# A fused attention and two-layer feed-forward kernel: all of w_in loaded ahead of w_out, and later keys and values loaded from GpSimd's queue

## The chip, the cores and the metric

One core of a Trainium2 chip runs the whole program. Times are device microseconds from start to end of one execution; the time of a kernel is the median of its runs. PE is TensorE (PEld its weight load), DVE is VectorE, ACT is ScalarE, POOL is GpSimd and SP is SyncE, which computes nothing here and starts DMA transfers. Each engine takes its own instructions strictly in order, and a transfer is started by an instruction in the queue of SP, ACT or POOL.

## The reference

Keys and values are averaged over groups of eight rows, then comes softmax attention, and two feed-forward layers follow it:

```python
B, H, S, D = 8, 8, 576, 64
k_p = k.reshape(B, H, 72, 8, D).mean(axis=3)
v_p = v.reshape(B, H, 72, 8, D).mean(axis=3)
attn = softmax(q @ k_p.transpose(0, 1, 3, 2) / sqrt(D))
x = (attn @ v_p) as 4608 tokens of 512
h = x @ w_in                         # 512 x 2048
x = (h * cos(h)) @ w_out             # 2048 x 512
g = x @ w_gate                       # 512 x 1536
out = (silu(g) * (x @ w_val)) @ w_out2
```

q, k and v are float32; the weights are float64.

## The kernel before

The program has two large stages. In the first, tokens go in nine blocks of 512 (`NB`), and each block in 16 slots (`NF1`): a slot computes 128 columns of h with twelve matmuls (`pe_h`, L507 to L509), its cosine on ACT and DVE (`turns`, `cosine`: L516, L518, L519, L540, L541, L544), and multiplies it with 128 rows of w_out into four accumulators (`pe_y`, L570 in block 0, L577 to L579 later). The attention of batch b + 1 is spread over slots of the blocks before it is needed. The second stage (the gate, value and output layers) is not touched here.

Ahead of slot 0 stands a prologue: the first batch's attention, written as a string of steps (`program`, L1057). In it `s`, `x`, `p`, `a` are scores, softmax, transposed probabilities and attention times values; `K0` to `K3` and `U0` are the second batch's sums of keys and values on DVE (L190, L192); `q` loads the second batch's q (four transfers, all on ACT's queue); `iN` loads N units of w_in, `oN` N units of w_out; `fN` takes N steps of weight conversion; `x4` is the softmax of the last tile; `k` prepares the second batch's keys; `b` starts the first load of batch 2's keys.

Weights are doubles and are turned into floats by hand: `cv_exp` (L445, takes the exponent), `cv_bias` (ACT, L451), `cv_sign` (L456), `cv_high` (L462), `cv_low` (L467), `cv_mul` (L473), and for w_in a split in a high and a low part (ACT L974, DVE L987). One unit of w_in or of w_out is 128 rows of 512 doubles, 512 KB; one of w_in comes as two transfers of 256 KB. The units are converted in a fixed sequence (`order`): w_in's first eight, then w_out's first, then one of w_in and one of w_out by turns. There are 16 of each. w_in's units are loaded straight into their homes (`wa00` to `wa33`), of which wa20 to wa22 and wa30 to wa33 hold the second batch's raw values and keys until their sums are done; w_out's units pass through two staging tiles (`raw`), so that the third waits for the first one's conversion.

From batch 2 on, keys and values come in 13 pieces a batch (8 of keys, 72 x 512 floats, 144 KB; 5 of values in two transfers each, 128 x 512 floats), through two tiles (tag `kv`, two buffers). `do_raw` starts the load of the next piece and then sums the present one on POOL (L190 twice, L192 once). Six batches make 108 such transfers. The sums of batch b go to a tile `kp` or `vp` that has one buffer, so they wait until PE has transposed the keys of the batch before (`prep_k`, L214), or until `prep_v` has read the values before. `prep_v(2)` writes into new tiles (`vmh_2`, `vml_2`, `vl2_2`), which POOL clears once with a MEMSET (L119); the one of `vmh_2` waits for PE's last use of the memory (L358), and ACT's L233 waits for that MEMSET.

The order of the instructions on each engine is set by the tile framework's scheduler when the program is built: it takes what is ready by its own estimates of time, and the written order as priority. On the chip the order is fixed.

Of the kernel before, what the change touches and what calls it, by code (L numbers as in the profile page):

```python
# [25 lines left out]
def fused_kernel(  # L26
# [18 lines left out]
    nc = tc.nc  # L45
# [7 lines left out]
    NP = H // 2  # L53
    SM = 64
# [102 lines left out]
    kview = [k[b].rearrange(pairs, r=2, l=POOL) for b in range(B)]  # L157
    vview = [v[b, :, : SM * POOL].rearrange(pairs, r=2, l=POOL) for b in range(B)]
    vleft = [v[b, :, SM * POOL :].rearrange("h (s l) d -> h s (l d)", l=POOL) for b in range(B)]

    def load_kv(b, kind, i):

        rows = SP if kind == "k" else P
        t = kvraw[b, kind, i] = p1a.tile([P, POOL * D], F32, name=f"{kind}raw_{b}_{i}", tag="kv", bufs=2)[:rows]
        if kind == "k":
            nc.sync.dma_start(t, kview[b][i % 2, :, i // 2])
        else:
            for r in range(2):
                nc.sync.dma_start(t[r * SM : (r + 1) * SM], vview[b][r, :, i] if i < NP else vleft[b])

    def load_kv1():

# [196 lines left out]
    def do_raw(b, i):  # L369
        at = (b - 2) * (H + NP + 1) + i  # L370
        if at + 1 < len(raws):
            load_kv(*raws[at + 1])
        sum_kv(*raws[at])
# [677 lines left out]
    def sum_v1():  # L1051
        new_vp(1)
        for j, t in vraw1:
# [1 line left out]


    program = (  # L1057
        "s0 s1 f4 x0 s2 p0 V0 v x1 p1 f3 s3 a0 x2 p2 f3 x3 i1 p3 a1 w F3 X s4 i1 q o2 "
        "K0 K1 K2 K3 U0 x4 k b i3 f6 "
    )  # L1060
    steps = {
        "s": s_,
# [11 lines left out]
        "q": lambda: load_q(1),  # L1074
        "k": lambda: prep_k(1),
        "b": lambda: load_kv(*raws[0]),
        "w": lambda: wo_raw.extend(
            p1w.tile([P, 8, DM], F32, name=f"wo_{i}", tag=f"big{i}", bufs=1) for i in range(2)
# [179 lines left out]
```

## Time and profile before

| | before |
|---|---|
| median of 3 runs | 1803.17 us (1802.95 to 1803.2) |
| the profiled execution | 1804.83 us, its span 1803.1 us |
| mean granted TensorE clock | 0.995 |
| PE busy | 1737.5 us (96%) |
| DVE, ACT, POOL busy | 1263.8 (70%), 1066.6 (59%), 171.7 (10%) |
| DMA | 357.01 MB, mean 198 GB/s |

The span is 1.7 us shorter than the execution, and the execution is 1.7 us longer than the median of the runs. PE's row in the profile's picture of 40 slices (45 us each) reads 2, 8, 7 and then nines: what PE does not use of the span lies in the first 130 us and in short gaps up to 320 us. In the same slices DVE reads 6 8 9 8 6 and POOL 0 1 5 0 5. A wait in the profile is put down to the instruction that ended it.

### The profile page before, as it was taken

The page shows a single profiled execution, that of the slowest core. Times are in us where ns is not written, and L with a number is a line of the kernel's source. Part 1 is how long each engine was busy: PE and PEld are TensorE (multiplying, and loading weights), DVE is VectorE, ACT ScalarE, POOL GpSimd, SP SyncE. Part 2 cuts the span into 40 slices and gives each one's busy share as a digit, 9 for nine tenths or more (in the row PEclk, how much of TensorE's full clock was granted, in tenths as well). Part 3 has the DMA queues.
Part 4 walks back from the last instruction along what each step waited for, and adds up shares of the span by engine and source line. Part 5 has one row for each costly group of instructions (what it writes and reads, how often), then busy time and mean ns, then how long its engine had stood idle before and what let it go on. Part 6 is the DMA issues. An engine that isn't in the chain of part 4 may idle for free.

```text
span 1803.1 us, 23421 instructions
## 1 busy us (share of the span) xinstructions
PE 1737.5 (96%) x8044; PEld 1439.4 (80%) x8044; DVE 1263.8 (70%) x2152; ACT 1066.6 (59%) x1933; POOL 171.7 (10%) x254
## 2 busy tenths in 40 slices
PE   2879999999999999999999999999999999999998
PEld 2546587888878888878877888888888888999998
DVE  6898688877877677787875586863584367358446
ACT  3578587777777767778776565533443344344333
POOL 0150513304104022000000000000000000000000
PEclk9989999999999999999999999999999999999999
DMA  9934246446566455474885488576667556787773
GB/s 186 203 104 120 79 165 188 156 131 197 148 205 218 114 198 144 158 220 153 235 275 176 159 320 291 193 252 225 194 200 267 193 192 221 290 265 246 294 249 93
DMA packets 248157, 357.01 MB, mean 198 GB/s; under 512 B 149608, under 2 KB 155752, under 8 KB 248040
## 3 DMA queue, kind: packets, MB, share of 16 engines
q1 hardware_dynamic: 224840, 352.58, 61.7%
q10 hardware_dynamic: 23200, 2.95, 1.1%
q8 instruction: 64, 1.05, 0.2%
q14 instruction: 53, 0.43, 0.1%
HBM read 285.74 MB, written 69.73 MB: 197 GB/s over the span
## 4 chain that ended last, share of the span: by engine, by line
PE 68%; DVE 14%; DMA 9%; ACT 5%; issue 2%; SPq 1%; POOL 0%; ACTq 0%; DVEq 0%
PE X L762 13%; PE oX L892 8%; PE Y L762 7%; PE h L507 4%; PE h L509 4%; PE h L508 4%; PE acc L578 4%; PE oY L892 4%; PE acc L579 4%; PE acc L577 4%; PE Z L762 3%; DMA w2r<-w_dram 2%; PE oZ L892 2%; PE av L358 2%; PE acc L570 2%
## 5 line engine op out<-in xcount | busy, mean ns | idle before, releaser
L762 PE MATMUL X<-t_P,wc 128*128 128x512 f32 (+1 forms) x1080 | 232.6, 367 | 1.0 <-ACT u L811 1.0
L507 PE MATMUL h<-xhl,wa 128*128 128x512 f32 x576 | 231.5, 402 | 0.0
L508 PE MATMUL h<-xhl,wa 128*128 128x512 f32 x576 | 226.3, 393 | 1.3 <-DVE xhl L131 1.3
L509 PE MATMUL h<-xhl,wa 128*128 128x512 f32 x576 | 225.6, 392 | 0.0
L762 PEld LDWEIGHTS X<-t_P,wc 128*128 128x128 f32 x1080 | 196.5, 188 | 27.5 <-ACT u L811 2.4
L578 PE MATMUL acc<-gl,wo_ring 128*128 128x512 f32 x448 | 176.4, 394 | 1.7 <-DVE gl L558 1.5
L577 PE MATMUL acc<-gh,wo_ring 128*128 128x512 f32 x448 | 175.1, 401 | 3.1 <-ACT gh L555 2.9
L579 PE MATMUL acc<-gh,wo_ring 128*128 128x512 f32 x448 | 175.4, 391 | 0.0
L544 DVE SCALAR_TENSOR_TENSOR w<-w,hs 128x512 f32<-128x512 f32 x144 | 102.3, 710 | 49.7 <-ACT w L541 48.4
L516 ACT ACTIVATE hs<-h 128x512 f32<-128x512 f32 x144 | 85.7, 595 | 76.4 <-DVE w L544 47.8
L540 ACT ACTIVATE w<-w 128x512 f32<-128x512 f32 x144 | 91.0, 632 | 64.9 <-DVE w L519 63.8
L507 PEld LDWEIGHTS h<-xhl,wa 128*128 128x128 f32 x576 | 108.7, 189 | 25.7 <-issue 4.1
L508 PEld LDWEIGHTS h<-xhl,wa 128*128 128x128 f32 x576 | 108.7, 189 | 25.3 <-issue 2.4
L509 PEld LDWEIGHTS h<-xhl,wa 128*128 128x128 f32 x576 | 108.5, 188 | 23.8 <-issue 0.9
L519 DVE SCALAR_TENSOR_TENSOR w<-w,hs 128x512 f32<-128x512 f32 x144 | 105.3, 731 | 23.7 <-ACT w L518 23.5
L814 DVE TENSOR_TENSOR p<-p,X 128x512 f32<-128x512 f32 (+1 forms) x60 | 37.9, 632 | 117.0 <-PE X L762 109.5
L558 DVE TENSOR_TENSOR gl<-w,gh 128x512 fp32r<-128x512 f32 x128 | 90.9, 710 | 40.2 <-ACT gh L555 38.6
L130 ACT CAST xhl<-pst 128x1024 fp32r<-128x1024 f32 (+1 forms) x70 | 67.7, 967 | 71.3 <-PE oX L892 26.1
L518 ACT ACTIVATE w<-hs,few 128x512 f32<-128x512 f32 x144 | 104.5, 725 | 7.3 <-DMA w_dram<-ce_w 4.2
L892 PE MATMUL oX<-xhl,wc 128*128 128x512 f32 (+1 forms) x480 | 102.8, 368 | 0.0
L578 PEld LDWEIGHTS acc<-gl,wo_ring 128*128 128x128 f32 x448 | 84.6, 189 | 21.5 <-DVE gl L558 5.2
L577 PEld LDWEIGHTS acc<-gh,wo_ring 128*128 128x128 f32 x448 | 84.1, 189 | 21.7 <-ACT gh L555 4.9
(197 smaller groups left out, 3586.3 us busy)
## 6 DMA issues: line engine op xcount, KB each, us to landing
wc<-wc_dram SPq DMA_DIRECT2D x273, 512.0 KB
wo_ring<-wo_dram SPq DMA_DIRECT2D x112, 512.0 KB
wc_dram<-wc SPq DMA_DIRECT2D x42, 512.0 KB
wc_dram<-ow SPq DMA_DIRECT2D x42, 256.0 KB
y_dram<-yo SPq DMA_DIRECT2D x18, 512.0 KB
w_dram<-ce_w SPq DMA_DIRECT2D x36, 256.0 KB
st_i<-in_moe_w_in_dram SPq DMA_DIRECT2D x32, 256.0 KB
st_o<-in_moe_w_out_dram SPq DMA_DIRECT2D x16, 512.0 KB
```

What stands on the lines that cost most here:

```text
L507: nc.tensor.matmul(ps, whi, xhl[:, 0, c], start=c == 0, stop=False)
L508: nc.tensor.matmul(ps, whi, xhl[:, 1, c], start=False, stop=False)
L509: nc.tensor.matmul(ps, wlo, xhl[:, 0, c], start=False, stop=c == KC - 1)
L518: nc.scalar.activation(w, h, AF.Identity, bias=magic)
L519: nc.vector.scalar_tensor_tensor(out=w, in0=w, scalar=MAGIC, in1=h, op0=ALU.subtract, op1=ALU.subtract)
L540: nc.scalar.activation(w, w, AF.Sin, scale=PI)
L544: nc.vector.scalar_tensor_tensor(out=w, in0=w, scalar=1.0, in1=h, op0=ALU.subtract, op1=ALU.mult, reverse0=True)
L577: nc.tensor.matmul(acc[n][i], a[:, cols], xh, start=f == 0, stop=False)
L578: nc.tensor.matmul(acc[n][i], a[:, cols], xl, start=False, stop=False)
L579: nc.tensor.matmul(acc[n][i], b[:, cols], xh, start=False, stop=f == NF1 - 1)
L762: nc.tensor.matmul(ps[:, :hb], w, t[:, x, c, :hb], start=first and c == 0 and n == 0, stop=c == 1 and n == 2, skip_group_check=not first,)
L892: nc.tensor.matmul(banks[key][m][:, :hb], u, x[:, b, i, :hb], start=first_ and j == i == k == 0, stop=j == NJ - 1 and i == 1 and k == 2, s ...
```

## The change

Three lines change. The step `i11` loads all that is left of w_in behind the second batch's sums and ahead of `o2`, which before stood ahead of the sums with `i3` behind `b`; the loads that the slots of block 0 issued one by one find nothing left to do. And `load_kv`, which loads the pieces of keys and values of batches 2 to 7, issues from POOL's queue and not from SP's.

```diff
     def load_kv(b, kind, i):
         rows = SP if kind == "k" else P
         t = kvraw[b, kind, i] = p1a.tile([P, POOL * D], F32, ..., tag="kv", bufs=2)[:rows]
         if kind == "k":
-            nc.sync.dma_start(t, kview[b][i % 2, :, i // 2])
+            nc.gpsimd.dma_start(t, kview[b][i % 2, :, i // 2])
         else:
             for r in range(2):
-                nc.sync.dma_start(t[r * SM : (r + 1) * SM], vview[b][r, :, i] if i < NP else vleft[b])
+                nc.gpsimd.dma_start(t[r * SM : (r + 1) * SM], vview[b][r, :, i] if i < NP else vleft[b])
...
     program = (
-        "s0 s1 f4 x0 s2 p0 V0 v x1 p1 f3 s3 a0 x2 p2 f3 x3 i1 p3 a1 w F3 X s4 i1 q o2 "
-        "K0 K1 K2 K3 U0 x4 k b i3 f6 "
+        "s0 s1 f4 x0 s2 p0 V0 v x1 p1 f3 s3 a0 x2 p2 f3 x3 i1 p3 a1 w F3 X s4 i1 q "
+        "K0 K1 K2 K3 U0 i11 o2 x4 k b f6 "
     )
```

SP's queue behind w_in's eighth unit (`st_i1_3`), before. `st_o0_0` and `st_o0_1` are w_out's first two units, `kraw_2_0` the first keys of batch 2, `st_i2_0` w_in's ninth unit; `DMAHW` names the semaphore of an earlier transfer that has to have landed.

```order
L438 DMA st_i1_3_432<-in_moe_w_in_dram 64x512 [waits DMAHW6_49]
L438 DMA st_o0_0_440<-in_moe_w_out_dram 128x512 [waits DMAHW7_49]
L438 DMA st_o0_1_442<-in_moe_w_out_dram 128x512 [waits DMAHW0_49]
L166 DMA kraw_2_0_479<-in_k_dram 72x512 [waits DMAHW1_49]
L438 DMA st_i2_0_481<-in_moe_w_in_dram 64x512 [waits DMAHW2_49,DVE_49]
L438 DMA st_i2_0_481<-in_moe_w_in_dram 64x512 [waits DMAHW3_49]
```

The same queue in the changed kernel, where units `st_i2_0` to `st_i3_1` follow on `st_i1_3` with the waits that `st_o0_0` and the rows behind it had; `st_i3_2` waits for DMAHW4 in its first half, and then come:

```order
L438 DMA st_i3_2_481<-in_moe_w_in_dram 64x512 [waits DMAHW5_49]
L438 DMA st_i3_3_484<-in_moe_w_in_dram 64x512 [waits DMAHW6_49]
L438 DMA st_i3_3_484<-in_moe_w_in_dram 64x512 [waits DMAHW7_49]
L438 DMA st_o0_0_487<-in_moe_w_out_dram 128x512 [waits DMAHW0_49]
L438 DMA st_o0_1_489<-in_moe_w_out_dram 128x512 [waits DMAHW1_49]
L438 DMA st_o0_2_610<-in_moe_w_out_dram 128x512 [waits DMAHW2_49,DMAHW0_49,DVE_49]
L438 DMA st_o0_3_670<-in_moe_w_out_dram 128x512 [waits DMAHW3_49,DMAHW1_49,DVE_49]
```

The eight last units of w_in have gone ahead of w_out's first, and the keys and values are gone from the queue, here and in all that follows; w_out's units stand one behind the other.

DVE at the end of the prologue, before: exponents of w_in's eighth unit, of w_out's first two, the conversion of w_in's seventh, and exponents of its ninth and tenth.

```order
L445 TENSOR_SCALAR ce_i1_3_495<-st_i1_3_432 128x512 [waits DMAHW6_49,DMAHW4_49]
L445 TENSOR_SCALAR wo_0_392<-st_o0_0_440 128x512 [waits DMAHW7_49,PE_49]
L445 TENSOR_SCALAR wo_0_392<-st_o0_1_442 128x512 [waits DMAHW0_49]
L456 SCALAR_TENSOR_TENSOR ce_i1_2_399<-st_i1_2_364,ce_i1_2_399 128x512 [waits Activation_49]
L462 TENSOR_SCALAR st_i1_2_364<-st_i1_2_364 128x512 [waits DVE_49]
L467 SCALAR_TENSOR_TENSOR st_i1_2_364<-st_i1_2_364 128x512 [waits DVE_49]
L473 SCALAR_TENSOR_TENSOR ce_i1_2_399<-st_i1_2_364,ce_i1_2_399 128x512 [waits DVE_49]
L445 TENSOR_SCALAR wo_1_393<-st_i2_0_481 128x512 [waits DMAHW3_49,DMAHW2_49]
L445 TENSOR_SCALAR wo_1_393<-st_i2_1_484 128x512 [waits DMAHW6_49,DMAHW5_49]
```

The same place in the changed kernel.

```order
L445 TENSOR_SCALAR ce_i1_3_510<-st_i1_3_432 128x512 [waits DMAHW6_49,DMAHW4_49]
L445 TENSOR_SCALAR wo_1_393<-st_i2_0_463 128x512 [waits DMAHW7_49,DMAHW0_49]
L456 SCALAR_TENSOR_TENSOR ce_i1_2_399<-st_i1_2_364,ce_i1_2_399 128x512 [waits Activation_49]
L462 TENSOR_SCALAR st_i1_2_364<-st_i1_2_364 128x512 [waits DVE_49]
L467 SCALAR_TENSOR_TENSOR st_i1_2_364<-st_i1_2_364 128x512 [waits DVE_49]
L445 TENSOR_SCALAR wo_1_393<-st_i2_1_466 128x512 [waits DMAHW2_49,DMAHW1_49]
L473 SCALAR_TENSOR_TENSOR ce_i1_2_399<-st_i1_2_364,ce_i1_2_399 128x512 [waits DVE_49]
L445 TENSOR_SCALAR wo_1_393<-st_i2_2_469 128x512 [waits DMAHW5_49,DMAHW3_49]
L445 TENSOR_SCALAR wo_1_393<-st_i2_3_472 128x512 [waits DMAHW7_49,DMAHW6_49]
```

The four units of w_in from the ninth to the twelfth take the place of w_out's two; w_out's first is met 35 rows later, behind block 0's first cosine product (L544), and PE's first product with w_out comes behind the fourth group of h and not ahead of it.

POOL after the keys of batch 2 have been used (the two L192 wait for that on PE), before: the MEMSET of `vmh_2` stands ahead of the sums of batch 3's keys.

```order
L192 TENSOR_TENSOR kp_3_1565<-kraw_3_0_1423 72x64 [waits PE_49]
L192 TENSOR_TENSOR kp_3_1565<-kraw_3_1_1563 72x64 [waits Pool_49]
L119 MEMSET vmh_2_1461 128x512 [waits PE_49]
L190 TENSOR_TENSOR kraw_3_2_1615<-kraw_3_2_1615 72x256 [waits DMAHW7_49,Pool_49]
L190 TENSOR_TENSOR kraw_3_2_1615<-kraw_3_2_1615 72x128 [waits Pool_49]
L192 TENSOR_TENSOR kp_3_1565<-kraw_3_2_1615 72x64 [waits Pool_49]
```

The end of the same piece in the changed kernel, from the 18th row behind the same two L192 on.

```order
L166 DMA kraw_3_7_1964<-in_k_dram 72x512 [waits Pool_49]
L190 TENSOR_TENSOR kraw_3_6_1882<-kraw_3_6_1882 72x256 [waits DMASW0_49]
L190 TENSOR_TENSOR kraw_3_6_1882<-kraw_3_6_1882 72x128 [waits Pool_49]
L192 TENSOR_TENSOR kp_3_1565<-kraw_3_6_1882 72x64 [waits Pool_49]
L169 DMA vraw_3_0_2025<-in_v_dram 64x512 [waits Pool_49]
L169 DMA vraw_3_0_2025<-in_v_dram 64x512
L190 TENSOR_TENSOR kraw_3_7_1964<-kraw_3_7_1964 72x256 [waits DMASW1_49]
L190 TENSOR_TENSOR kraw_3_7_1964<-kraw_3_7_1964 72x128 [waits Pool_49]
L192 TENSOR_TENSOR kp_3_1565<-kraw_3_7_1964 72x64 [waits Pool_49]
L169 DMA vraw_3_1_2091<-in_v_dram 64x512 [waits Pool_49]
L169 DMA vraw_3_1_2091<-in_v_dram 64x512
L119 MEMSET vmh_2_1461 128x512 [waits PE_49]
```

The sums of all keys of batch 3, six loads of keys and four of values have come ahead of the MEMSET of `vmh_2`, for which ACT's L233 waits. The first two loads of keys (`kraw_2_0`, `kraw_2_1`), which stood on SP behind w_out's second and w_in's fourteenth unit, now stand on POOL behind its first MEMSETs and wait for nothing.

## Rows read from the trace of the kernel before

**Rows 1.** Who made PE wait between 85 and 360 us: total us, times, longest.

```profile
PE acc L570 <- DVE w L544: 9.2, 4, 4.4
PE acc L570 <- DVE wo L473: 3.4, 3, 2.4
PE acc L578 <- DVE gl L558: 2.7, 2, 1.5
```

**Rows 2.** Busy us by stretch: length, PE, PEld, DVE, ACT, POOL, clock, DMA, GB/s.

```profile
0.00:25.00 25.00, 1.05 (x5) 0.89 (x6) 11.70 (x19) 4.66 (x7) 4.46 (x19) 1.00 0.99 181
85.00:131.00 46.00, 36.82 (x128) 22.80 (x128) 45.61 (x71) 33.07 (x80) 31.16 (x40) 0.89 0.43 115
131.00:194.00 63.00, 62.34 (x228) 37.40 (x226) 48.12 (x96) 51.05 (x124) 0.59 (x2) 1.00 0.36 99
194.00:214.00 20.00, 16.57 (x47) 8.21 (x46) 18.98 (x27) 9.22 (x19) 16.42 (x19) 1.00 0.29 92
```

**Rows 3.** DVE's L544 from 85 to 131 us, then from 131 to 194: mean ns.

```profile
L544 DVE SCALAR_TENSOR_TENSOR w<-w,hs 128x512 f32<-128x512 f32 x5 | 4.7, 946 | 0.0
...
L544 DVE SCALAR_TENSOR_TENSOR w<-w,hs 128x512 f32<-128x512 f32 x9 | 6.2, 688 | 4.2 <-ACT w L541 4.2
```

**Rows 4.** DVE in order of time, start of the span: start, us, what, wait.

```profile
11.47 1.22 DVE L190 TENSOR_TENSOR kst<-kst 72x1024 f32<-72x1024 f32 x1 [3.93 <-DMA kst<-in_k_dram]
```

**Rows 5.** DVE in order of time, the stretch of the second place above.

```profile
64.66 0.43 DVE L445 TENSOR_SCALAR wo<-st_o 128x512 uint32<-128x512 uint32 x1 [0.53 <-DMA st_o<-in_moe_w_out_dram]
66.40 0.43 DVE L445 TENSOR_SCALAR wo<-st_o 128x512 uint32<-128x512 uint32 x1 [1.31 <-DMA st_o<-in_moe_w_out_dram]
...
70.41 0.43 DVE L445 TENSOR_SCALAR wo<-st_i 128x512 uint32<-128x512 uint32 x1 [0.41 <-DMA st_i<-in_moe_w_in_dram]
72.52 0.43 DVE L445 TENSOR_SCALAR wo<-st_i 128x512 uint32<-128x512 uint32 x1 [1.68 <-DMA st_i<-in_moe_w_in_dram]
```

**Rows 6.** SP's queue in order of time, 60 to 80 us, and at 198.

```profile
60.52 0.84 SPq L438 DMA_DIRECT2D st_o<-in_moe_w_out_dram  x2
61.41 0.40 SPq L166 DMA_DIRECT2D kraw<-in_k_dram  x1
...
69.27 1.52 SPq L438 DMA_DIRECT2D st_i<-in_moe_w_in_dram  x2
77.77 1.75 SPq L438 DMA_DIRECT2D st_i<-in_moe_w_in_dram  x3
...
198.39 1.76 SPq L166 DMA_DIRECT2D kraw<-in_k_dram  x2
```

**Rows 7.** POOL in order of time, four places.

```profile
85.07 3.24 POOL L190 TENSOR_TENSOR kraw<-kraw 72x256 f32<-72x256 f32 x2 [5.14 <-DMA kraw<-in_k_dram]
...
179.11 0.59 POOL L192 TENSOR_TENSOR kp<-kraw 72x64 f32<-72x64 f32 x2 [50.26 <-PE kps L214]
194.35 0.52 POOL L119 MEMSET vmh<- 128x512 f32 x1 [14.65 <-PE av L358]
...
202.12 1.84 POOL L190 TENSOR_TENSOR kraw<-kraw 72x256 f32<-72x256 f32 x2 [2.29 <-DMA kraw<-in_k_dram]
```

**Rows 8.** All of POOL's L190 on keys: ns min/median/max.

```profile
L190 POOL TENSOR_TENSOR kraw<-kraw x96: 453/788/2707, 67.9 to 678.9; 72x256 f32<-72x256 f32 x48, 72x128 f32<-72x128 f32 x48
```

**Rows 9.** ACT in order of time, at its wait for the MEMSET.

```profile
198.33 0.85 ACT L233 ACTIVATE vmh<-vp 64x256 fp32r<-64x256 f32 x2
...
201.76 0.72 ACT L518 ACTIVATE w<-hs,few 128x512 f32<-128x512 f32 x1 [1.84 <-PE acc L570]
```

**Rows 10.** DVE in order of time, w_out's fourteenth unit.

```profile
194.47 0.69 DVE L544 SCALAR_TENSOR_TENSOR w<-w,hs 128x512 f32<-128x512 f32 x1 [0.54 <-ACT w L541]
...
204.17 0.68 DVE L519 SCALAR_TENSOR_TENSOR w<-w,hs 128x512 f32<-128x512 f32 x1
...
208.38 0.67 DVE L473 SCALAR_TENSOR_TENSOR wo<-st_o,wo 128x512 f32<-128x512 f32 x1
```

**Rows 11.** PE in order of time, its product with that unit.

```profile
209.11 3.70 PE L570 MATMUL acc<-w,wo 128*128 128x512 f32 x8 [2.40 <-DVE wo L473]
```

## The prediction

> **What bounds the kernel now.** The profile's table says that PE is busy for 96% of the span, so the first question is where the other 4% lie. The waits of PE [rows 1] name the stages: between 85 and 360 us PE waits 9.2 us for DVE's cosine products (L544) and 3.4 us for converted units of w_out (L473), 15.3 us in all with the 2.7 us of L558. Before 85 us PE waits for the prologue, which is DVE's work. Behind 330 us PE has no gaps, so a change to the loads there can lengthen nothing that PE sees. So I price the change in the first 330 us alone.
>
> The stretches [rows 2] say what PE waits for. From 85 to 131 us DVE is busy 45.61 of 46 us, with POOL's 31.16 us of sums beside it: DVE is the bound. From 131 to 194 us PE is the bound (62.34 of 63), and POOL rests. One kind of instruction read in both shows what POOL costs DVE: L544 takes 946 ns with POOL at work and 688 ns without [rows 3]. If all of DVE stretches so, the first stretch holds 45.6 x (1 - 688/946) = 12.4 us of stretch, or 12.4/40 = 0.31 us for each POOL instruction. From 194 to 214 us both are at work again (18.98 and 16.42 of 20 us).
>
> **The change part by part.** The sum is made on the profiled execution (1804.83 us), which is 1.7 us above the median; I assume the same difference for the changed kernel.
>
> *The start.* The first two loads of keys (2 x 144 KB) leave SP and stand early on POOL, where they wait for nothing. They run beside the loads for which DVE waits 3.93 us at 11.47 [rows 4]. At the 181 GB/s of the first 25 us [rows 2] they take 295 KB / 181 = 1.6 us of transfer. The bounds are 0 (they go in gaps, the DMA engines being shared packet by packet) and +1.6; I take **+1.0**.
>
> *w_in ahead of w_out.* Before, DVE waited 0.53 and 1.31 us for w_out's first two units and 0.41 and 1.68 us for w_in's ninth and tenth, 3.9 us in all [rows 5]. SP issued the last of these units early, but from 69.27 + 1.52 to 77.77 it stood still [rows 6], behind the semaphore of the fourth transfer of q. In the changed order 12 transfers of w_in (3072 KB) stand ahead of that wait, where 3472 KB stood: w_out's two units, a load of keys and nine transfers of w_in. A unit of 512 KB follows the last one by 2.11 us (70.41 to 72.52 [rows 5]), so 400 KB are 1.6 us less in front of q's last landing. DVE also has work in hand where it waited: 3.9 us of waits can shrink. But DVE then meets q's fourth transfer too, in the middle of this work and not behind it. The bounds are -1.9 (half of the waits) and +0.2 (q lands as late as now and DVE waits for it); I take **-1.1**. w_out's first unit now lands behind two units of w_in, which SP starts when q has landed: 77.8 + 3 x 2.11 = 84.1 us or up to 1.5 us later. DVE meets it 35 rows later than before, at about 86 us, so I cost it at nothing; the cover is those 35 rows, and if it fails the price is the delay, 1 to 2 us.
>
> *Sums that leave the bound stretch.* The first keys land earlier, so the pair of L190 at 85.07 (3.24 us [rows 7]) goes ahead of the stretch that DVE bounds. Its share of the stretch is 3.24/31.16 x 12.4 = 1.3 us. Bounds -1.3 and 0, since it may run beside other DVE work that counts: **-1.0**.
>
> *Issues that enter it.* POOL now starts 18 transfers itself between 85 and 134 us (6 of batch 2's keys, 10 of values, the first 2 of batch 3's keys). The trace has no load that POOL starts. At 0.31 us each, as for one of its sums, DVE would lose 18 x 0.31 = 5.6 us; at nothing, as the MEMSET at 194.35 [rows 7] beside which L544 keeps 0.69 us [rows 10], it loses none. Starting a transfer reads no tile, as the MEMSET reads none, so I stay near that end: **+0.5**. Starting loads also lengthens POOL's own queue, which nobody waits for before the next place.
>
> *The MEMSET of vmh_2.* This is the place that decides. On POOL the MEMSET stood right behind batch 3's first two sums and was done at 194.87 [rows 7]. Now it stands behind six sums of keys, six loads of keys and four of values, which may begin at 179.7, when PE has released the sums. ACT's L233 waits for the MEMSET [rows 9]; behind it stand L518 on ACT, DVE's L519 and w_out's fourteenth unit, for which PE waits 2.40 us [rows 9 to 11]. Let c be POOL's time for starting one transfer. The first pair lands 3.7 us after its issue (198.39 [rows 6] to 202.12 [rows 7]); a piece's sum takes 2.1 us beside little else (1.84 and an L192 of about 0.3); eight starts stand in the chain behind the first landing; the MEMSET takes 0.5. So it ends at 179.7 + 3.7 + 6 x 2.1 + 8c + 0.5 = 196.5 + 8c, less what overlaps.
>
> For c the lower bound is 0.40, SP's time for the same load (61.41 [rows 6]); the upper is 1.58, a whole pair of L190 on such a tile, 2 x 0.788 [rows 8]. I take one L190, 0.79, between them. Then the MEMSET ends at 202.8. In the trace L233 begins at 198.33, and L518 ends at 202.48 because PE releases its tile late [rows 9]. Without that wait, L518 ends 0.85 us (L233) + 0.74 (what lies from 199.18 to the wait's start at 199.92) + 0.72 = 2.3 us after L233's start, so at 205.1; DVE's L519 starts there and not at 204.17 [rows 10], and the unit is ready 4.9 us later as before (204.17 to 209.05): 210.0 where it was 209.05. PE waits 0.9 us more there, and the other two waits for w_out (3.4 - 2.4 = 1.0 us [rows 1]) have their cover back, since the unit behind has been converted meanwhile: **0**. With c = 0.40 the MEMSET is no bound, and since most sums have moved to 183 to 197 us, where DVE has slack, the wait of 2.4 us can go: -2.4. With c = 1.58 the MEMSET ends at 209.1 and the unit at 216.3, 7.2 us late, less the 1.0: +6.2. Each 0.1 us of c is 0.8 us.
>
> *Batch 4's sums.* At 300 and 320 us PE waits 2.7 us by L558 [rows 1], while POOL sums. POOL's own issues can move those sums either way: **0**, bounds -1.5 and +1.5.
>
> **Sum:** 1.0 - 1.1 - 1.0 + 0.5 + 0 + 0 = -0.6 us, so 1804.2 us for a profiled execution and 1803.17 - 0.6 = **1802.6 us** as a median.
>
> **The rivals.** *POOL's starts are dear (slower).* If c is well above 1 us, ACT stands at L233 for the MEMSET, and the slot's cosine, w_out's conversion and PE stand behind it. At c = 1.58 that is 1802.6 + 6.2 = 1808.8 us. For it speaks that POOL's sums stretch beside DVE (453 ns at the least, 2707 at the most [rows 8]), and that DVE is busy 18.98 of 20 us there [rows 2]; against it, that SP starts the same load in 0.40 us and that DVE has slack up to 194 us. It decides from c = 1.3 on, where 8 x (1.3 - 0.79) = 4.1 us less 0.6 reach 3.6 us, which is 0.2%. The page "SBUF — State Buffer" of the Trainium skill (section "SBUF: two separate sides") speaks for this rival: it says that for a load issued from GpSimd that engine's cores write the descriptors, and cannot while a DVE instruction in a two-port mode holds the port that they share. Its section "A bandwidth-pool intuition that's wrong (but worth ruling out)" gives about 620 ns for such a transfer alone and about 3100 ns beside DVE; with c = 3.1 the sum would be 1802.6 + 8 x 2.3 = 1821 us, an estimate by that page, which no run here shows yet.
>
> *Starts are cheap (faster).* With c at 0.40, the place at 209 us gives 2.4; w_in's order gives its full 1.9 and the starts cost DVE nothing: -0.6 - 2.4 - 0.8 - 0.5 = -4.3, so 1798.9 us. For it speaks that DVE idles 3.9 us in the prologue for transfers that the new order brings earlier; against it, that POOL is the engine whose sums already stretch.
>
> *The reorder moves nothing.* If q's fourth transfer still lands at 77.7, DVE and SP both stand at it and the reorder's gain is +0.2 and not -1.1: 1803.9 us.
>
> **How the numbers follow.** No change can be told from one of 0.2%, 3.6 us: 1799.6 to 1806.8. The forecast has 0.32, the reorder that moves nothing 0.08: both fall within, 0.40. Dear starts have 0.34, since half of the way from 0.40 to 1.58 and more lies above 1 us and DVE's share there is high. Cheap starts have 0.26. The range reaches beyond both rivals' points, to c = 1.8 above (1802.6 + 8 x 1.0 = 1811) and to 1798 below, and leaves 0.2 out: 1798 to 1811.
>
> **What would show it.** POOL's rows will show c: one start near 0.8 us. The MEMSET of vmh_2 should end near 202.8 and ACT's L233 follow it; PE's wait for the fourteenth unit should be 3.3 us. DVE's waits for transfers from 60 to 80 us should shrink from 3.9 to near 2, with q's last transfer among them. L544's mean from 85 to 131 us should stay near 946 ns; if it is 1050 or more, the starts stretch DVE. At 11.47 DVE should come 1 us later. I would be wrong at the root if PE showed new waits behind 330 us, or if its waits for w_out grew because its first unit came after 87 us.

## The result, and the profile after

The changed kernel takes 1823.22 us (median of 4 runs, 1819.31 to 1825.09) against 1803.18 us: a ratio of 1.0103, with a 95% interval of 1.0088 to 1.0119. It is 20 us slower, where within 0.2% was forecast and the range ended at 1811. The profiled execution took 1823.94 us, its span 1822.2.

The page's first part, busy time, share of the span and instructions of each engine; before, DVE had 1263.8 us and POOL 171.7:

```profile
PE 1742.4 (96%) x8044; PEld 1440.8 (79%) x8044; DVE 1281.1 (70%) x2152; ACT 1067.0 (59%) x1933; POOL 232.9 (13%) x362
```

DVE has the same 2152 instructions and is busy 17.3 us longer. POOL has 108 more, the starts, and is busy 61 us longer. The longest waits of PE between 85 and 360 us (total us, times, longest), which answer to [rows 1]:

```profile
PE acc L570 <- DVE w L544: 10.1, 3, 3.9
PE acc L570 <- DVE wo L473: 3.9, 2, 2.3
PE acc L577 <- ACT gh L555: 2.5, 1, 2.5
PE acc L578 <- DVE gl L558: 1.9, 3, 0.9
```

They add up to 18.4 us, where [rows 1] add up to 15.3.

Busy time by stretch in the changed kernel (length, PE, PEld, DVE, ACT, POOL, clock, DMA share, GB/s), as in [rows 2], with two stretches behind 330 us:

```profile
0.00:25.00 25.00, 0.71 (x4) 0.53 (x4) 10.68 (x17) 4.52 (x7) 10.14 (x25) 1.00 0.96 180
85.00:131.00 46.00, 37.48 (x142) 24.55 (x141) 45.79 (x79) 36.54 (x87) 37.28 (x45) 0.93 0.36 112
131.00:194.00 63.00, 59.50 (x201) 35.48 (x200) 48.85 (x92) 46.02 (x110) 10.83 (x19) 0.92 0.40 108
194.00:214.00 20.00, 19.95 (x67) 10.94 (x66) 14.83 (x21) 13.09 (x30) 17.23 (x29) 1.00 0.37 108
400.00:450.00 50.00, 47.69 (x221) 38.49 (x220) 42.78 (x60) 32.63 (x64) 35.03 (x55) 1.00 0.54 165
500.00:560.00 60.00, 54.89 (x243) 43.96 (x243) 47.50 (x74) 39.30 (x73) 35.94 (x57) 0.97 0.63 196
```

The last two in the kernel before:

```profile
400.00:450.00 50.00, 50.00 (x242) 42.18 (x241) 39.12 (x70) 37.28 (x68) 18.10 (x27) 1.00 0.64 199
500.00:560.00 60.00, 58.85 (x265) 48.14 (x265) 42.71 (x75) 42.25 (x80) 10.81 (x16) 1.00 0.73 237
```

The surprise is behind 330 us. From 400 to 450 us PE loses 2.3 us, and DVE does 60 instructions in 42.78 us, where it did 70 in 39.12. POOL has twice the work in the same 50 us.

To see where the time goes, I compare the start of the same matmul in two traces: the first L508 (the second of the three that make up h's products) of a slot, counting the slots from 0 through the nine blocks. The table gives how much later it starts than in the kernel before, in us, and with it the timed ratio of each run. Each ratio compares with runs of the kernel before on the same chip; those reached from 1797.6 to 1809.8 us, so ratios are used and not times. The slots are read from one execution of each kernel, the ratio from all of its runs; one of e11's eleven runs took 2490.6 us, at a mean granted clock of 0.664, and is left out of its ratio.

| kernel | slot 0 | 4 | 8 | 16 | 32 | 48 | 64 | 143 | DVE busy | ratio, 95% interval |
|---|---|---|---|---|---|---|---|---|---|---|
| start in the kernel before | 73.6 | 106.6 | 147.9 | 204.8 | 322.8 | 424.3 | 527.8 | 1007.8 | 1263.8 | |
| changed kernel | 5.2 | 4.5 | 10.2 | 9.9 | 10.0 | 14.2 | 20.0 | 18.0 | 1281.1 | 1.0103 (1.0088 to 1.0119) |
| e1, order alone | 1.8 | 0.9 | 1.8 | 1.2 | 1.3 | 1.3 | 1.3 | -0.8 | 1263.6 | 1.0022 (1.0003 to 1.0041) |
| e2, queue alone | 2.2 | 5.1 | 3.5 | 4.1 | 5.6 | 8.8 | 15.8 | 12.4 | 1282.5 | 1.0073 (1.0053 to 1.0093) |
| e3, first two on SP | 1.5 | 3.5 | 8.9 | 8.7 | 10.2 | 13.6 | 20.1 | 17.7 | 1283.8 | 1.0105 (1.0081 to 1.0130) |
| e4, starts doubled | 6.3 | 7.2 | 12.3 | 13.5 | 15.6 | 15.9 | 18.6 | 17.1 | 1279.6 | 1.0087 (1.0065 to 1.0108) |
| e7, keys alone | 3.2 | 7.2 | 8.8 | 9.9 | 9.2 | 10.2 | 12.3 | 8.5 | 1272.1 | 1.0074 (1.0049 to 1.0100) |
| e5, SP, no L190 | -0.8 | -2.4 | -9.6 | -10.3 | -18.3 | -18.3 | -19.6 | -24.4 | 1228.8 | 0.9881 (0.9858 to 0.9905) |
| e6, queue, no L190 | 2.5 | 1.1 | -6.8 | -7.4 | -14.9 | -14.9 | -16.0 | -22.5 | 1229.5 | 0.9907 (0.9880 to 0.9934) |
| e9, queue, one buffer | 3.2 | 0.4 | 1.7 | 2.3 | 0.4 | 0.6 | 2.5 | -2.5 | 1260.8 | 0.9984 (0.9967 to 1.0001) |
| e13, queue, copy | 3.3 | 4.9 | 6.2 | 5.7 | 10.3 | 10.4 | 13.2 | 10.2 | 1262.6 | 1.0046 (1.0030 to 1.0063) |
| e14, copy, one buffer | 1.6 | 0.5 | -4.5 | -3.6 | -2.4 | -2.1 | 2.7 | 2.3 | 1260.3 | 0.9995 (0.9982 to 1.0008) |
| e10, SP, one buffer | 2.2 | 5.0 | 4.4 | 8.5 | 14.2 | 14.2 | 22.1 | 26.3 | 1258.6 | 1.0146 (1.0129 to 1.0162) |
| e11, changed, one buffer | 3.1 | -0.1 | -2.2 | -1.8 | -5.6 | -5.5 | -3.3 | -5.7 | 1262.8 | 0.9988 (0.9977 to 1.0000) |
| e12, e9 with first on SP | 0.0 | -1.2 | -4.1 | -4.5 | -9.0 | -8.9 | -7.3 | -11.1 | 1262.9 | 0.9964 (0.9951 to 0.9976) |
| e16, e11 with first on SP | 2.5 | -0.7 | -0.2 | 0.3 | -3.4 | -3.3 | -1.6 | -6.7 | 1263.2 | 1.0000 (0.9985 to 1.0014) |

### The profile page after: what moved, and what is told of

Its sections match the earlier page's. It is cut to its first block, busy times and chain, and to the rows that moved or that the text cites. A ratio compares the mean times of both kernels' runs of the same rounds, so it can differ in the third digit from the quotient of the medians.

```text
span 1822.2 us, 23374 instructions
## 1 busy us (share of the span) xinstructions
PE 1742.4 (96%) x8044; PEld 1440.8 (79%) x8044; DVE 1281.1 (70%) x2152; ACT 1067.0 (59%) x1933; POOL 232.9 (13%) x362
## 4 chain that ended last, share of the span: by engine, by line
PE 68%; DVE 17%; ACT 7%; DMA 6%; issue 2%; SPq 0%; ACTq 0%; DVEq 0%
PE X L762 15%; PE oX L892 8%; PE Y L762 8%; PE oY L892 4%; PE Z L762 4%; PE h L507 4%; PE h L509 4%; PE h L508 4%; PE acc L578 4%; PE acc L579 4%; PE acc L577 3%; PE oZ L892 2%; PE acc L570 2%; DVE w L519 2%; DVE w L544 2%
## 5 line engine op out<-in xcount | busy, mean ns | idle before, releaser
L508 PE MATMUL h<-xhl,wa 128*128 128x512 f32 x576 | 225.5, 391 | 2.6 <-DVE xhl L131 2.5
L544 DVE SCALAR_TENSOR_TENSOR w<-w,hs 128x512 f32<-128x512 f32 x144 | 104.0, 722 | 49.3 <-ACT w L541 47.8
L516 ACT ACTIVATE hs<-h 128x512 f32<-128x512 f32 x144 | 85.9, 596 | 79.7 <-DVE w L544 48.8
L508 PEld LDWEIGHTS h<-xhl,wa 128*128 128x128 f32 x576 | 108.7, 189 | 26.8 <-DVE xhl L131 3.8
L519 DVE SCALAR_TENSOR_TENSOR w<-w,hs 128x512 f32<-128x512 f32 x144 | 104.7, 727 | 27.0 <-ACT w L518 26.9
L577 PEld LDWEIGHTS acc<-gh,wo_ring 128*128 128x128 f32 x448 | 84.4, 189 | 24.4 <-ACT gh L555 7.4
```

The source lines that it names most:

```text
L508: nc.tensor.matmul(ps, whi, xhl[:, 1, c], start=False, stop=False)
L519: nc.vector.scalar_tensor_tensor(out=w, in0=w, scalar=MAGIC, in1=h, op0=ALU.subtract, op1=ALU.subtract)
L544: nc.vector.scalar_tensor_tensor(out=w, in0=w, scalar=1.0, in1=h, op0=ALU.subtract, op1=ALU.mult, reverse0=True)
L577: nc.tensor.matmul(acc[n][i], a[:, cols], xh, start=f == 0, stop=False)
```

## The experiments

### Which of the two edits

e1 has only the new string, e2 only the new queue. e3 is the changed kernel with batch 2's first two loads of keys back on SP. e4 is e2 with each load started in two halves of 256 columns.

```diff
 e3   if kind == "k":
-         nc.gpsimd.dma_start(t, kview[b][i % 2, :, i // 2])
+         first = b == 2 and i < 2
+         (nc.sync if first else nc.gpsimd).dma_start(t, kview[b][i % 2, :, i // 2])
 e4   if kind == "k":
-         nc.gpsimd.dma_start(t, kview[b][i % 2, :, i // 2])
+         for c in (slice(0, 256), slice(256, 512)):
+             nc.gpsimd.dma_start(t[:, c], kview[b][i % 2, :, i // 2][..., c])
```

(e4's values likewise.)

> Only the program's string is changed; keys and values are still loaded from SP's queue. The changed kernel is 20 us slower than the one before. Its PE starts slot 0 of block 0 5.2 us later, of which 2.0 us stand at DVE's wait for the first keys (11 to 17 us) and 3.2 us at DVE's waits for w_in's ninth unit. Theory O (the order of the loads costs most): about 1815 us or more, with a slot 0 that is 3 us late and the half-clock stretch near 145 us there too. Theory Q (the queue costs most): 1804 to 1809 us; slot 0 late by 3 us, hardly anything behind it, and the wait at 17 us gone.

> Only load_kv issues from GpSimd's queue; the program's string is that of before. Theory Q (POOL's starts, 0.53 us each with 0.29 us ahead of each, draw its sums out and disturb DVE and ACT at every batch's sums): 1814 to 1820 us, with losses at slots 30 to 64 as in the changed kernel (some 10 us by then) and a slot 0 that is 2 us late from the two early loads. Theory O: 1804 to 1808 us.

> The changed kernel with only the first two loads of batch 2's keys put back on SP. If those two early loads cost the start 2.0 us (DVE's second wait for the first keys, 1.83 us at 16.85), slot 0 comes 2 us earlier and the kernel takes 1821 us; if their transfers only moved a wait that is late anyway, 1823 us. A theory in which the sums of these two pieces, done early, spare DVE a stretch later gives 1823 to 1826 us.

> As the run with the queue alone, but each load from GpSimd's queue is started as two halves of 256 columns: 216 starts instead of 108, the same bytes. If the starts on POOL are what costs, the loss against the kernel before about doubles where the sums stand (each piece's chain on POOL is 0.5 to 1.1 us longer): 10 us or more above the run with the queue alone. If it is where the transfers or the sums stand in time, and not the starts, within 3 us of it.

The order costs 0.22% (0.03 to 0.41) and the queue 0.73% (0.53 to 0.93); within the intervals their sum is the 1.03% of both. So theory Q holds for most of it. e3 gains 3.7 us at slot 0 and has lost it again by slot 32: what is late at the start is hidden later by what is late anyway. e4 speaks against the starts by themselves: 108 more of them move the ratio by 0.14%, about 2.5 us and not 10, which is less than the intervals of e2 and e4 can tell from nothing, while DVE's busy time does not grow.

### What a start costs by itself

POOL's starts of the keys' loads in the changed kernel: ns min/median/max.

```profile
L166 POOL DMA_DIRECT2D kraw<-in_k_dram x48: 525/528/706, 4.4 to 670.2; - x48
```

0.53 us each, with 0.29 us of waiting for the sum ahead of it. e5 and e6 take the two L190 of each piece away, on SP's and on POOL's queue:

```diff
-        while h > D:
+        while h > D and eng is not nc.gpsimd:
             eng.tensor_add(raw[..., :h], raw[..., :h], raw[..., h : 2 * h])
```

> The kernel before without the two L190 of each piece of keys and values of batches 2 to 7 on POOL: L192 alone is left, so the averages are wrong sums of two groups. Loads from SP's queue as before. It is the base of the next run. If POOL's sums stretch DVE as the trace of before shows, it takes 1798 to 1803 us, with DVE busy some 30 us less than 1264.

> The same without L190, but with the loads started from GpSimd's queue and the program's string of before. Theory S (the 108 starts themselves slow DVE or PE): 8 to 13 us above the run on SP's queue without L190, as with the sums. Theory N (the starts cost nothing alone, and what costs is a sum that stands right behind a start and so takes DVE's instructions by surprise): 0 to 4 us above it, 2 of them from the two early loads, with DVE busy within 3 us of that run.

Without L190 DVE is busy 1228.8 and 1229.5 us: 108 starts stretch DVE by nothing that can be seen. The time differs by 0.26%, some 4.7 us, of which 3.3 us stand at slot 0 already; that is a little more than the 4 us that theory N allowed and far less than theory S asked for. e5 also shows what the sums on POOL cost the kernel before: 1.2%, some 21 us, where 1798 to 1803 us were expected and 1780.59 were measured.

### What stands behind a start

DVE in the changed kernel, in order of time, and POOL beside it:

```profile
427.84 0.69 DVE L467 SCALAR_TENSOR_TENSOR st_w<-st_w 128x512 f32<-128x512 uint32 x1
428.56 1.62 DVE L473 SCALAR_TENSOR_TENSOR ce_w<-st_w,ce_w 128x512 f32<-128x512 f32 x1
430.10 0.95 DVE L519 SCALAR_TENSOR_TENSOR w<-w,hs 128x512 f32<-128x512 f32 x1
432.41 1.48 DVE L544 SCALAR_TENSOR_TENSOR w<-w,hs 128x512 f32<-128x512 f32 x1 [1.36 <-ACT w L541]
```

```profile
427.81 1.04 POOL L169 DMA_DIRECT2D vraw<-in_v_dram  x2 [0.30 <-POOL kp L192]
428.87 1.63 POOL L190 TENSOR_TENSOR vraw<-vraw 128x256 f32<-128x256 f32 x2
430.58 0.65 POOL L192 TENSOR_TENSOR vp<-vraw 128x64 f32<-128x64 f32 x1
431.53 1.04 POOL L169 DMA_DIRECT2D vraw<-in_v_dram  x2 [0.29 <-POOL vp L192]
```

L467 runs wholly beside two starts and takes 0.69 us, as alone. L473 begins beside a start and is still running when L190 follows that start: 1.62 us, and L544 the same way 1.48. Over all of DVE's instructions that began between 80 and 720 us I took each one's excess over the lower quartile of its form (line, operation and shape), and sorted them by what POOL did beside them. "Behind a start" means that a POOL instruction began within 0.06 us of the end of a start; a DVE instruction that met several kinds is counted with the sums behind a start first, then with other sums.

| kernel | beside starts alone | beside sums behind a start | beside other sums |
|---|---|---|---|
| before | | | 286 instructions, 39.9 us |
| changed | 62, -0.1 us | 63, 28.1 us | 223, 29.5 us |
| e2 | 57, 0.0 | 58, 29.7 | 216, 29.9 |
| e9, one buffer | 109, 0.1 | 2, 0.0 | 325, 38.0 |
| e13, copy | 64, 0.0 | 71, 0.1 | 273, 38.7 |

A sum right behind a start stretches a DVE instruction by 446 ns on the average in the changed kernel and 513 in e2 (449 in e7, 367 in e4), another sum by 117 to 142. The excess beside sums of both kinds is 17.7 us above that of the kernel before in the changed kernel and 19.7 in e2, and DVE is busy 17.3 and 18.7 us longer.

The single instructions show what happens. In the changed kernel 38 of DVE's instructions were running when an L190 began right behind a start. 27 of them were lengthened by more than 200 ns, and 24 of these ended either 0.29 us (8) or 0.56 us (16) behind the end of that L190, though they had begun 0.09 to 0.43 us before it: they were held until it was done. Those with one input were held too (an L445 took 1.40 us, alone 0.42). In e9 66 instructions of DVE were running when the first L190 of a piece began after a wait for its transfer, and none was lengthened by more than 16 ns; there it was the L190 that could take longer, 0.72 to 4.73 us. So what changes behind a start is which of the two gives way.

e7 has the sums behind a start for the keys alone. e9 and e13 take them away in two ways: e9 with one buffer for the raw pieces, so that a sum waits for its own transfer, and e13 with an instruction of POOL between.

```diff
 e9
-            ... tag="kv", bufs=2)[:rows]
+            ... tag="kv", bufs=1)[:rows]
 e7
-                nc.gpsimd.dma_start(t[r * SM : (r + 1) * SM], vview ...)
+                nc.sync.dma_start(t[r * SM : (r + 1) * SM], vview ...)
 e13  def pool_sum(eng, dst, raw):
         h = POOL * D // 2
+        if eng is nc.gpsimd:
+            eng.tensor_copy(raw[..., :1], raw[..., :1])
```

> The run with the queue alone, but only the keys' 48 loads come from GpSimd; the values' 60 stay on SP. If the loss goes with the starts, 48/108 of the 13 us, so 1809 us with the 2 us at the start among them; if it goes with pieces whose sum stands behind a start (48 of 78 pieces), 1811 us; if it is made at the ends of blocks (slots 32, 48 and 64), where values are summed, 1806 to 1808 us.

> The run with the queue alone, but one buffer for the raw pieces instead of two, so that a piece's sum waits for its own transfer and doesn't stand right behind a start; 108 starts and all sums stay. Theory N: DVE busy falls from 1282.5 towards 1264 us and the time from 1819 to 1806 to 1813 us. Theory S: the time stays at 1816 us or above. If the sums' mere spread over the slots costs, it grows, since they end later.

> The run with the queue alone, with its two buffers, all starts and all sums, and one small instruction more: POOL copies one column of a piece onto itself ahead of the piece's first L190, so that no L190 stands right behind a start. Theory N (an L190 right behind a start holds DVE's instruction that runs there until it ends): DVE's stretch beside such sums goes, DVE busy falls from 1282.5 to 1264 to 1272 us and the time from 1819 to 1804 to 1812 us. If one buffer helped because it spreads the sums out in time, and not because of what stands behind a start, the time stays at 1816 us or above, since here nothing is spread out.

e7 missed all three of its expected times: it loses as much as e2 (1.0074), but elsewhere, 7.2 us by slot 4 and little behind slot 16. So the loss goes neither with the count of starts nor with the count of pieces. e9 gains all of the queue's loss, more than the 6 to 13 us that were expected of theory N, and DVE's busy time is back. In e13 the start is followed by the copy (start, us):

```profile
96.59 0.54 POOL L166 DMA_DIRECT2D kraw<-in_k_dram  x1 [0.30 <-POOL kp L194]
97.13 0.70 POOL L190 COPY kraw<-kraw 72x1 f32<-72x1 f32 x1
97.90 1.96 POOL L192 TENSOR_TENSOR kraw<-kraw 72x256 f32<-72x256 f32 x2
```

The copy does to DVE's stretch just what was expected: 0.1 us are left beside 71 instructions, and DVE is busy 1262.6 us. But the time falls from 1.0073 to 1.0046 only, some 5 of 13 us, and not to 1804 to 1812. Either the stretch is not the whole cost, or the copies have a price of their own.

At one place they have one. It is the chain of the MEMSET of `vmh_2` that the prediction called the place that decides (POOL, ACT and PE in e13, whose lines from the copy on are numbered two higher):

```profile
210.20 0.55 POOL L119 MEMSET vmh<- 128x512 f32 x1
210.78 0.85 ACT L235 ACTIVATE vmh<-vp 64x256 fp32r<-64x256 f32 x2 [5.73 <-POOL vmh L119]
218.22 9.63 PE L572 MATMUL acc<-w,wo 128*128 128x512 f32 x16 [5.31 <-DVE wo L475]
```

Six copies stand ahead of that MEMSET and with the gaps behind them take 2.4 us. ACT waited 5.73 us for it, and PE 5.31 us for the unit of w_out behind it, where it waited 2.34 in the changed kernel and 2.36 in e2. So 2 to 3 of the 8 us that e13 still loses are probably the copies' own, an estimate from these rows, and 3.3 us stand at slot 0 already.

### How close the sums stand

What POOL waited for ahead of its first L190 of a piece, between 60 and 720 us (us, times): before, in the changed kernel, in e9 and in e13 (there the copy's line).

```profile
  DMA kraw<-in_k_dram: 197.0, 25
  DMA vraw<-in_v_dram: 49.6, 26
```

```profile
  DMA kraw<-in_k_dram: 27.7, 15
  DMA vraw<-in_v_dram: 18.9, 13
```

```profile
  DMA kraw<-in_k_dram: 120.2, 47
  DMA vraw<-in_v_dram: 89.5, 30
```

```profile
  DMA kraw<-in_k_dram: 23.3, 14
  DMA vraw<-in_v_dram: 12.9, 9
```

Before, POOL waited 246.6 us for its pieces, because their loads stood on SP among everything else that SP does. With the loads on POOL and two buffers it waits 46.6 us: sum follows on sum, and most pieces of a batch fall on the same few slots. One buffer spaces them out again (209.7 us). To ask whether this closeness costs anything beside the stretch behind starts, I compare the stretch from 400 to 450 us in seven kernels:

| kernel | POOL busy, us | excess of all of DVE's instructions, us | PE busy, us | later from slot 32 to slot 48, us |
|---|---|---|---|---|
| before | 18.10 | 3.2 | 50.00 | |
| changed | 35.03 | 10.3 | 47.69 | 4.2 |
| e2 | 35.52 | 11.3 | 48.48 | 3.2 |
| e7 | 29.20 | 8.4 | 49.67 | 1.0 |
| e4 | 32.71 | 5.8 | 49.93 | 0.3 |
| e13 | 37.49 | 5.5 | 50.00 | 0.1 |
| e9 | 21.19 | 4.6 | 50.00 | 0.2 |

```profile
400.00:450.00 50.00, 50.00 (x240) 41.72 (x239) 41.35 (x70) 35.59 (x67) 37.49 (x64) 1.00 0.59 188
```

The line is e13's. Its POOL is the busiest of all, and PE loses nothing: here the loss goes with DVE's stretched instructions and not with how close the sums stand.

e14 has both the copy and one buffer:

> The run with the small copy, with one buffer instead of two. With two buffers the copy took DVE's stretch behind the starts away (DVE busy 1262.6 us) and gave back 5 of the 13 us; one buffer without it gave all. If the rest is the density of the sums (two buffers let POOL sum piece after piece, one makes each wait for its transfer), this run takes 1800 to 1804 us, as the one with one buffer alone. If the rest is what the 78 copies themselves cost, 1810 us or more.

0.9995 against e13's 1.0046: with the copies, the second buffer costs 0.51%, some 9 us. e14 is 0.11% above e9, within the intervals, but that does not price the copies of e13: with one buffer POOL waits for each piece in any case, and in e14 the MEMSET of `vmh_2` stands ahead of the last sums of keys (at 200.09) and not behind them. So taking the second buffer away takes back all of the queue's 0.73% (e9). The stretch behind the starts alone is worth some 0.27% (e2 to e13, two ratios whose intervals overlap a little), and more if the copies cost what the rows above suggest. How the rest divides between the copies' price, the two early loads and the closeness of the sums is not shown.

e10 is the other half of the test, one buffer with the loads on SP; e11 is the changed kernel with one buffer, e12 is e9 with batch 2's first load on SP, and e16 is e11 with that.

```diff
 e12, e16
-            nc.gpsimd.dma_start(t, kview[b][i % 2, :, i // 2])
+            (nc.sync if (b, i) == (2, 0) else nc.gpsimd).dma_start(t, kview[b][i % 2, :, i // 2])
```

> The kernel before with one buffer for the raw pieces instead of two, and nothing else: loads from SP. It tells whether one buffer is good whatever the queue. Theory N (a sum right behind a start is the cost, which loads from SP don't have): there is little to gain here, 1800 to 1806 us. If fewer sums in a row spare DVE in any case, it gains on the kernel before as the run with one buffer gained on the queue alone: 1790 us.

> The changed kernel with one buffer for the raw pieces. Theory N: most of the 13 us of the queue and of the 5 us that queue and order cost together (the half-clock stretch near 145 us) go: 1803 to 1809 us, the order's 1 to 4 us and the start's 2 us left. If the 5 us come from the order of w_in and w_out on DVE, 1808 to 1814 us.

> The run with the queue alone and one buffer, and batch 2's first load of keys put back on SP, so that nothing of it runs beside the start's loads. Slot 0 was 3.2 us late there; it should come 2 to 3 us earlier, and the time should be 1798 to 1801 us, below both kernels. If the late slot 0 has another cause, or DVE's stretch between 85 and 131 us takes the gain back, 1802 us as without it.

> The changed kernel with one buffer and batch 2's first load of keys on SP. With the string of before that kernel was 0.36% faster than the one before. If the order of w_in and w_out costs by itself what it cost with loads from SP (0.22%), this one is 1798 to 1802 us; if it costs nothing once the sums are spread out, 1794 to 1798 us.

e10 missed both expectations: 1.46% slower. Its SP queue's waits (total us, times, longest) say why:

```profile
SPq L166 <- POOL kp L192: 110.2, 37, 15.3
SPq L169 <- POOL vp L192: 56.4, 24, 3.5
```

In the kernel before SP waited 48.8 us at L166 for the same L192. A load that waits for its one buffer holds everything behind it on SP; the lateness grows by steps up to slot 64 and on. On POOL's queue the same wait holds POOL's own work alone. So the queue and the number of buffers belong together: POOL's queue is bad with two buffers and good with one, SP's the other way round.

e11 is the plainest test: the changed kernel, with one buffer and nothing else changed, takes 1801.0 us, below both of its expected ranges, and its ratio of 0.9988 (0.9977 to 1.0000) takes back all of the 1.03%.

e12 is faster than both kernels: 0.9964 (0.9951 to 0.9976). Two stretches of e12 and the same two of the kernel before:

```profile
85.00:125.00 40.00, 34.32 (x117) 21.58 (x117) 38.61 (x69) 32.32 (x79) 20.25 (x27) 0.87 0.29 90
150.00:194.00 44.00, 43.89 (x166) 27.40 (x165) 31.96 (x59) 35.38 (x87) 18.86 (x27) 1.00 0.46 122
```

```profile
85.00:125.00 40.00, 30.82 (x105) 18.68 (x105) 39.61 (x62) 30.32 (x75) 28.33 (x37) 0.89 0.48 128
150.00:194.00 44.00, 44.00 (x167) 27.30 (x165) 29.77 (x59) 34.20 (x83) 0.59 (x2) 1.00 0.41 106
```

POOL's sums have left the stretch that DVE bounds (28.33 to 20.25 us) for one in which DVE has slack (0.59 to 18.86 us), DVE gets 69 instructions done in the first where it got 62, and PE loses 0.1 us in the second.

e16 against e12 is the price of the new order of w_in and w_out when the sums do not disturb: 1.0000 against 0.9964, 0.36%, which is at the upper end of what e1 left open. e16 missed both of its expected ranges (1805.0 us), and putting the first load on SP did not gain there on e11 (0.9988), where it gained in e12 on e9 (0.9984); why is open.

## Why the prediction was wrong

**The frame failed.** "Behind 330 us PE has no gaps, so a change to the loads there can lengthen nothing that PE sees": slots 32 to 64 lost 10 us of the changed kernel's 20. It was not quite true as a reading either, since PE was busy 58.85 of the 60 us from 500 on. That PE waits for nothing says that the others are in time with this work beside them; how little they have to spare it does not say. The loads decide when POOL sums and what stands ahead of each sum, and the sums hold DVE: from 400 to 450 us its instructions were stretched by 10.3 us where they had been by 3.2. The rival that starts are dear was looked for at one MEMSET, when the right place was every batch's sums. Of the 10 us ahead of slot 32, 5.2 stand at slot 0 (the next two terms bear on it) and 5.7 more came between slots 4 and 8. The latter hold PE's wait of 3.50 us for L544 at 145.00, and ahead of it DVE's L544 at 130.44, L519 at 134.13 and L456 at 136.89 took 1.72, 1.27 and 1.38 us beside sums behind starts, where 0.68 is usual.

**The start:** +1.0, bounds 0 and +1.6. DVE's second wait for the first keys is new, and all behind it is 2 us late:

```profile
16.85 1.22 DVE L190 TENSOR_TENSOR kst<-kst 72x1024 f32<-72x1024 f32 x1 [1.83 <-DMA kst<-in_k_dram]
```

Right mechanism, mis-sized term: 2.0. But it costs the end next to nothing where DVE is late for other reasons (e3), and 0.20%, some 3.6 us, where it is not (e12 against e9).

**w_in ahead of w_out:** -1.1, bounds -1.9 and +0.2; slot 0 came 1.8 us later in e1. DVE's waits for transfers in e1:

```profile
64.83 0.43 DVE L445 TENSOR_SCALAR wo<-st_i 128x512 uint32<-128x512 uint32 x1 [1.57 <-DMA st_i<-in_moe_w_in_dram]
69.82 0.43 DVE L445 TENSOR_SCALAR wo<-st_i 128x512 uint32<-128x512 uint32 x1 [2.78 <-DMA st_i<-in_moe_w_in_dram]
72.10 0.43 DVE L445 TENSOR_SCALAR wo<-st_i 128x512 uint32<-128x512 uint32 x1 [1.25 <-DMA st_i<-in_moe_w_in_dram]
74.31 0.43 DVE L445 TENSOR_SCALAR wo<-st_i 128x512 uint32<-128x512 uint32 x1 [1.78 <-DMA st_i<-in_moe_w_in_dram]
```

7.4 us of waits, where 3.9 stood and 2 were expected; in the changed kernel itself they are 8.6 (4.93, 0.38, 1.31 and 1.93). The step that failed is the count in KB. I took w_in's 2.11 us for a unit of w_out too, though [rows 5] show w_out's second 1.74 us behind its first. The fourth unit is there at 74.31, where it was at 72.52 [rows 5]: with w_out's two units among the four the same bytes came sooner than with four of w_in. w_in's units come as two transfers of 64 rows each; whether that is the reason no run tested. No row shows DVE waiting for q's last transfer, the mishap that set the upper bound.

**Sums that leave the bound stretch:** -1.0. Two pairs of L190 did leave it, but from 85 to 131 us L544 still took 909 ns on the mean where it took 946 [rows 3], and POOL was busier than before. The gain was used up by what follows.

```profile
L544 DVE SCALAR_TENSOR_TENSOR w<-w,hs 128x512 f32<-128x512 f32 x5 | 4.5, 909 | 0.0
```

**Starts that enter it:** +0.5, bounds 0 and 5.6. The question was put too narrowly. A start alone costs DVE 0.0 us, so the choice of the MEMSET's end for it was right; what was not asked is what the start does to the sum behind it. That is the cost the prediction put at nothing: 28.1 us on 63 of DVE's instructions, 17.7 us net of what other sums no longer cost.

**The MEMSET of vmh_2:** 0 at c = 0.79. The term came out right, c did not: it is 0.53. Three rows of POOL, and one each of ACT and PE:

```profile
189.28 0.59 POOL L192 TENSOR_TENSOR kp<-kraw 72x64 f32<-72x64 f32 x2 [48.90 <-PE kps L214]
...
209.43 1.04 POOL L169 DMA_DIRECT2D vraw<-in_v_dram  x2 [0.29 <-POOL kp L192]
210.47 0.54 POOL L119 MEMSET vmh<- 128x512 f32 x1
```

```profile
211.04 0.84 ACT L233 ACTIVATE vmh<-vp 64x256 fp32r<-64x256 f32 x2 [1.45 <-POOL vmh L119]
```

```profile
219.52 4.99 PE L570 MATMUL acc<-w,wo 128*128 128x512 f32 x11 [2.34 <-DVE wo L473]
```

From the end of L192 (189.87) to that of the MEMSET (211.01) are 21.1 us; the working gives 16.8 + 8 x 0.53 = 21.0 with the c that was measured. ACT waited 1.45 us for it and PE waited 2.34 us where it had waited 2.40 [rows 11]. So the working up to the MEMSET's end was right. The 0 was partly luck: by the prediction's own rule, 0.8 us for each 0.1 us of c, c = 0.53 should have taken some 2 us off PE's wait, and it took nothing.

**The Trainium skill's figure.** The estimate of 1821 us by the Trainium skill's page "SBUF — State Buffer" lies near the measured time, and not for its reason. That figure of the Trainium skill is the time of a transfer beside a copy on DVE, and the prediction put it in for POOL's time for a start. No start here took 3100 ns, but 516 to 706, also between 85 and 131 us, where DVE was busy 45.79 of 46 us. The transfers landed 3.2 us after their starts in the median; the prediction read 3.7 for a pair from SP. Another section of that page of the Trainium skill, "Who interferes with whom", says that a DVE instruction with two inputs in SBUF contends with a GpSimd instruction that reads SBUF. The trace agrees: L190 beside L544 and L473 stretches them, starts beside them do not. Why a sum behind a start makes DVE give way, and a sum after a wait does not, no row shows; the runs only show that an instruction of POOL between the two ends it.

What stays open: where e13's remaining 0.46% comes from beyond the copies and slot 0, and why e2 and e7 lose the same time in different places; each run also orders the other engines' instructions anew. Both kernels also show stretches at a granted clock of half (1.2 of 2.4 GHz) about PE's waits; in the changed kernel the longest one lies at PE's wait of 3.5 us, from 141.5 to 145.0:

```profile
143.90:154.10 10.20, 9.10 (x14) 3.93 (x15) 6.83 (x16) 4.78 (x11) 0.00 (x0) 0.50 0.12 45
```

How much such stretches cost beside the waits that they come with, busy times bound roughly: PE's same 8044 matmuls were busy 1737.5 us before and 1742.4 in the changed kernel (1743.4 in e13), so 4.9 of the 19.1 us by which the span grew are matmuls that took longer, and 14.2 are idle time of PE.

## What to carry to other kernels

A queue also paces: before moving loads from a queue where they stand in line to one where they don't, ask what their late arrival was keeping apart, what the starts will stand in front of, and choose the number of buffers for the new queue anew. That the bounding engine shows no gaps in a stretch is no proof that work may be moved into it; look at how full the engine is that feeds it. Before a transfer's place is priced in KB, take the time per unit of that very shape from the trace.

## What the runs showed of the hardware

A load started on POOL takes 0.53 us of POOL (516 to 706 ns) and stretches no instruction of DVE that runs beside it (0.1 us in all at most, over 57 to 109 instructions). A sum that begins within 0.06 us of a start's end holds most of the DVE instructions that are running (27 of 38 in the changed kernel) until it is done; the DVE instructions beside such sums take 446 and 513 ns longer on the average, over 63 and 58 of them; other sums lengthen one by 117 to 142 ns; a copy of one column between the two brings the excess to 0.1 us over 71 instructions. Where a sum begins after a wait for its transfer (e9), DVE's running instruction keeps its time within 16 ns, over 66 cases. Two L190 for each of 78 pieces, on an engine that is busy for a tenth of the span, cost this kernel 1.2% of its time.
